# Attention and a two-layer mixer on one core: scores computed in four quarters of the array, a pair's value products in one run, other PSUM banks, and filler products at the start

## The chip, the cores and the metric

The kernel runs on one core of a Trainium2 chip. Times are microseconds (us) of device time for one execution of the whole program. TensorE is called PE here, VectorE DVE, ScalarE ACT, GpSimd POOL; SP is the engine that issues the transfers. Each engine works through its own list of instructions in order.

## The reference

64 heads (8 batches of 8) of 576 positions and 64 dimensions; attention is causal in blocks of 64 positions. Then a mixer over positions and a two-layer network over 512 channels.

```
scores = scale * np.matmul(q, k.transpose(0, 1, 3, 2))
mask = block_i >= block_j                      # blocks of 64 positions
scores = np.where(mask, scores, -1000000000.0)
attn = softmax(scores); out = np.matmul(attn, v)
...
h = xt @ U @ V;  u = x + h.transpose(0, 2, 1)
ch = np.maximum(u @ w_ch1, 0.0) @ w_ch2
return u + ch
```

## The kernel before, in words

The work goes by pairs of heads, 32 pairs in all; four pairs make one batch. The queries of a head are cut into five tiles that end at positions 64, 192, 320, 448 and 576 (tile 0 has 64 queries, tiles 1 to 4 have 128), so tile i sees the first 128i+64 keys. For a pair p the steps are:

- `load_qk`, `load_v`: transfers; POOL scales the keys.
- `scores(p, s)`, twice per pair (s = 0, 1), called a score run here. PE multiplies queries by keys in float32. The two heads of the pair lie in rows 0 to 63 and 64 to 127 of the array, and a run takes tiles 4, 1 and 0 of one head and tiles 3 and 2 of the other, so that both halves work side by side. Tiles 4, 1 and 0 land in `bw` (two PSUM banks), tile 3 in `three`, tile 2 in `two`, a bank each. In tiles 1 to 4 the first 64 queries may not see the last 64 keys; a small bf16 product with the tile `mask` adds a large negative number there. DVE then takes the row maxima (L1215), ACT the exponentials with their sums (L1226).
- `normalise`: DVE inverts the sums, POOL scales the probabilities (L1250).
- `transpose`: PE turns the probabilities (L1293), ACT or DVE copies them out of PSUM (L1264, L1266). One copy in four goes to DVE (`VEC`).
- `apply_v(p, g)`: the value products (L1313) for the positions up to 320 (g = 0) and beyond (g = 1), each a task of its own; ACT copies the result to `xt`.
- `mix`: transposes (L1336), down product (L1351), up product (L1366) and the sum `u` (L1371). The largest |u| of a batch sets its scale (the product named `oneu`).

The network's work is cut in two. `ffn_chunk` (L666, L691) has 2304 products of 288 columns and runs in two banks `bf` between the attention's products; it needs the whole of batch 0 mixed and the first weights converted (DVE and ACT do that from raw words, with two products named `onew`). `block_products` (L915) has 3360 products and starts when the attention is over, because it takes over the attention's banks; its weights are prepared by ACT, DVE and POOL (L768).

What decides the order: every step is recorded with `add(engine, ns, prio, ...)`; `Plan.issue` then plays the tasks through with the costs written in the source and writes each engine's list in the order that this gives. A task starts there when its inputs are there, its engine is free, and each of its PSUM buffers finds a bank in its pool; among the ready ones the lowest `prio` goes first. FFN products have the highest number, so they fill what is left of PE. The attention's pools are `banks_a` (four banks), `banks_w` (`bw`), and for tile 3 of the first four pairs `banks_f` (`bf`), which the FFN uses later.

## Time and profile before

| | us |
|---|---|
| median of 3 runs | 1147.44 (1145.18 to 1148.29) |
| the profiled execution | 1149.23 |
| its span, first to last instruction | 1147.5 |
| first FFN product on PE | 115.3 |
| last product of the attention's last mix | 646.2 |
| last product of the FFN chunks | 737.5 |

The profiled execution took 1.7 us more than its span and 1.8 us more than the median of the runs. The span falls into a start, in which only the attention and the conversion of weights run; a long middle, in which FFN products fill PE between the attention's products; and the block products at the end. Busy times of an engine are unions of its instructions' spans; a PE product is shown from its start to the end of its pipeline, so neighbours overlap, and what a product costs PE is the distance of its start to the next one's.

### The profile page before, as it was taken

The page shows a single profiled execution, that of the slowest core. Times are in us where ns is not written, and L with a number is a line of the kernel's source. Part 1 is how long each engine was busy: PE and PEld are TensorE (multiplying, and loading weights), DVE is VectorE, ACT ScalarE, POOL GpSimd, SP SyncE. Part 2 cuts the span into 40 slices and gives each one's busy share as a digit, 9 for nine tenths or more (in the row PEclk, how much of TensorE's full clock was granted, in tenths as well). Part 3 has the DMA queues.
Part 4 walks back from the last instruction along what each step waited for, and adds up shares of the span by engine and source line. Part 5 has one row for each costly group of instructions (what it writes and reads, how often), then busy time and mean ns, then how long its engine had stood idle before and what let it go on. Part 6 is the DMA issues. An engine that isn't in the chain of part 4 may idle for free.

```text
span 1147.5 us, 24596 instructions
## 1 busy us (share of the span) xinstructions
PE 1096.5 (96%) x9088; PEld 875.1 (76%) x9088; DVE 875.0 (76%) x1946; ACT 653.0 (57%) x1666; POOL 351.0 (31%) x628
## 2 busy tenths in 40 slices
PE   5886998999999999999999999999999999999998
PEld 5665766778777877777878877777777777777777
DVE  4777887778775656567786572399999899999998
ACT  4666766676585756567577552154545554454544
POOL 3433433644563626264656755000000000000000
PEclk8887998999999999999999999999999999999999
DMA  3433553444423232233422431204031231404111
GB/s 106 131 101 98 160 163 107 148 148 122 146 85 105 77 116 75 96 129 115 140 84 63 117 102 47 78 1 125 16 111 52 73 95 31 117 13 120 33 53 43
DMA packets 68264, 107.32 MB, mean 94 GB/s; under 512 B 6896, under 2 KB 50928, under 8 KB 68144
## 3 DMA queue, kind: packets, MB, share of 16 engines
q1 hardware_dynamic: 68144, 105.75, 30.0%
q8 instruction: 72, 1.18, 0.4%
q14 instruction: 48, 0.39, 0.1%
HBM read 76.23 MB, written 29.49 MB: 92 GB/s over the span
## 4 chain that ended last, share of the span: by engine, by line
PE 82%; DVE 7%; ACT 5%; POOL 2%; issue 2%; DMA 1%; SPq 0%; ACTq 0%; POOLq 0%; DVEq 0%
PE bb L915 36%; PE bf L691 11%; PE bf L666 8%; PE ba L1293 7%; PE ba L1313 7%; PE bw L1191 6%; PE ba L1191 3%; DVE mx L1215 3%; ACT p L1226 3%; POOL p L1250 2%; PE ba L1336 1%; PE ba L1351 1%; PE ba L1366 1%; DMA st<-in_U_dram 1%; DMA raw<-in_qk_dram 0%
## 5 line engine op out<-in xcount | busy, mean ns | idle before, releaser
L1250 POOL TENSOR_SCALAR p<-p,rv 64x64 f32<-64x64 f32 (+4 forms) x384 | 187.6, 500 | 149.0 <-DVE rv L1239 58.8
L1215 DVE TENSOR_REDUCE mx<-bw 128x1 f32<-128x576 f32 (+2 forms) x192 | 79.4, 439 | 105.1 <-PE bw L1191 61.4
L915 PE MATMUL bb<-ph,w2h 128*128 128x288 f16 x560 | 151.0, 286 | 0.0
L915 PE MATMUL bb<-ph,w2l 128*128 128x288 f16 x560 | 151.0, 286 | 0.0
L915 PE MATMUL bb<-ph,w1h 128*128 128x288 f16 x560 | 148.7, 286 | 0.0
L915 PE MATMUL bb<-ph,w1l 128*128 128x288 f16 x560 | 148.7, 286 | 0.0
L1191 PE MATMUL bw<-raw 64*128 64x288 f32 (+2 forms) x512 | 132.4, 393 | 14.2 <-ACT p L1226 10.2
L837 ACT CAST ph<-hb 128x576 f16<-128x576 f32 x144 | 84.3, 590 | 82.8 <-PE bb L915 77.1
L915 PEld LDWEIGHTS <-w2h 128*128 128x128 f16 x1120 | 109.6, 98 | 27.5
L1226 ACT ACTIVATE p<-bw,mx 128x576 f32<-128x576 f32 (+2 forms) x192 | 93.4, 489 | 65.3 <-DVE mx L1215 46.8
L915 PEld LDWEIGHTS <-w1h 128*128 128x128 f16 x1120 | 109.6, 98 | 27.4
L915 PE MATMUL bb<-pl,w2h 128*128 128x288 f16 x560 | 123.5, 286 | 0.0
L1293 PE MATMUL ba<-ident,p 128*128 128x128 f32 x704 | 105.8, 284 | 12.7 <-ACT spare L1266 4.4
L915 PE MATMUL bb<-pl,w1h 128*128 128x288 f16 x560 | 114.4, 286 | 0.0
L691 PE MATMUL bf<-hh,w2h 128*128 128x288 f16 x384 | 110.9, 289 | 0.9 <-DVE ot L703 0.7
L1191 PEld LDWEIGHTS bw<-raw 64*128 64x128 f32 x512 | 85.0, 196 | 34.1 <-ACT p L1226 12.2
L691 PE MATMUL bf<-hl,w2h 128*128 128x288 f16 x384 | 110.6, 288 | 0.0
L691 PE MATMUL bf<-hh,w2l 128*128 128x288 f16 x384 | 110.6, 288 | 0.0
L1191 PE MATMUL ba<-raw 64*128 64x448 f32 (+1 forms) x240 | 103.8, 544 | 0.8 <-ACT xt L1266 0.8
L1293 PEld LDWEIGHTS ba<-ident,p 128*128 128x128 f32 x704 | 83.7, 146 | 21.4 <-POOL p L1250 8.3
L666 PEld LDWEIGHTS <-w1h 128*128 128x128 f16 x768 | 74.3, 98 | 23.3 <-issue 5.7
L839 DVE TENSOR_TENSOR pl<-hb,ph 128x576 f16<-128x576 f32 x144 | 91.1, 651 | 1.0
(167 smaller groups left out, 2465.3 us busy)
## 6 DMA issues: line engine op xcount, KB each, us to landing
raw<-in_qk_dram SPq DMA_DIRECT2D x31, 576.0 KB, 3.9
o_d<-ot SPq DMA_DIRECT2D x72, 144.0 KB, 1.8
vr<-in_v_dram SPq DMA_DIRECT2D x32, 320.0 KB, 3.2
ur<-u_d SPq DMA_DIRECT2D x64, 144.0 KB, 2.3
wr<-o_d SPq DMA_DIRECT2D x32, 288.0 KB, 3.0
out_dram<-wr SPq DMA_DIRECT2D x31, 288.0 KB, 2.3
st<-in_w_dram SPq DMA_DIRECT2D x16, 512.0 KB, 3.9
u_d<-ut SPq DMA_DIRECT2D x28, 288.0 KB, 2.3
```

Source lines behind the costliest of these rows:

```text
L666: nc.tensor.matmul(ps[:, :T], w()[wn][:, k, fs], m[k].ap, start=(i == 0), stop=(i == len(ops) - 1))
L691: nc.tensor.matmul(ps[:, :T], w()[wn][:, f, ms], hs[f][x].ap, start=(i == 0), stop=(i == len(ops) - 1))
L837: add("ACT", _act(n * T, True), E, lambda: nc.scalar.copy(h.ap[:, :n, :], x[0]()), [x[1]], [h])
L839: "DVE", _dve(n * T), E, lambda: nc.vector.tensor_sub(l.ap[:, :n, :], x[0](), h.ap[:, :n, :]), [x[1], h], [l],
L915: nc.tensor.matmul(bank[:, i, :T], x()[:, w(k)], p.ap[:, k, :], start=first and n == 0, stop=last and n == len(ops) - 1)
L1191: lambda: nc.tensor.matmul(out(), raw[r, qs], raw[r, S + k0 : S + k1], start=True, stop=not last),
L1215: lambda i=i, mx=mx: nc.vector.tensor_reduce(out=mx[: P if i else 64, i : i + 1], in_=view(i), op=ALU.max, axis=AX.XY if i == 4 else AX.X, ...
L1226: return nc.scalar.activation(out.rearrange("p (j k) -> p j k", j=2) if i == 4 else out, view(i), AF.Exp, bias=mx[:rows, i : i + 1], accum ...
L1250: lambda: nc.gpsimd.tensor_scalar(out=out, in0=x, scalar1=iv, scalar2=1.0, op0=ALU.mult, op1=ALU.mult),
L1293: nc.tensor.transpose(out=to, in_=pt_r[i][h % PB[i]][:, j * P : (j + 1) * P], identity=perm.ap)
L1313: nc.tensor.matmul(bank[64 * s : 64 * s + 64, x:n], vr[:, 5 * s + j, :], pw[s][:, _at(g, j)], start=(j == 0), stop=(j == NK[g] - 1),)
L1336: nc.tensor.transpose(out=ps[:, i, :], in_=xt[:, j * P : j * P + rows], identity=ident.ap)
```

## The change

Four things are changed, and the order follows from them.

1. The score products are cut by blocks of 64 queries. Each block of queries meets only the keys that it may see, and its product lands in PSUM rows 0 to 63 or 64 to 127, so that a run works in four quarters of the array (two heads by two halves of the output rows) instead of two halves. The products with `mask` go; the places that no product writes are filled with the large negative number once, at the start.
2. `apply_v` is one task per pair and takes two banks at once.
3. PSUM: tiles 2 and 3 get a pair of banks `bq` of their own; `banks_a` shrinks from four banks to two. For the first four pairs these two serve as a second pair for tiles 2 and 3 (class `Lent`), and transposes, values and mix use `bf`.
4. Order: scores get a lower priority number by `SL` = 1985, almost one pair; `normalise` is done per score run; `mx`, `ss` and `rv` have four slots; copies of transposes go to DVE only from pair 8 on (`VP`); the second half of the FFN's first weights gets a later priority (`WP2`, `WP4`). Where PE finds nothing ready in the planner's first 130 us and a bank `bf` is free, a product of a zero tile is written into the list (`idle`): bf16, 128 columns, with its own load of weights.

```diff
-PEQ = 1650.0
+PEQ = 1560.0
+PVX = 190.0
+NF = 4
+SL = 1985.0
+WARM = 130e3
+IDLE = 56.0
+VP = 8
...
-WP2, WP3, WP4 = 9000.0, 1000.0, 13000.0
+WP2, WP3, WP4 = 14000.0, 1000.0, 18000.0
...
                 if n is None:
+                    if e == "PE" and now < WARM and idle():
+                        busy[e] = True
+                        heapq.heappush(events, (now + IDLE, 0, -1, e))
                     continue
...
-    banks_a = [psa.tile([P, 512], F32, name=f"ba{i}") for i in range(6 - FB)]
+    banks_a = [psa.tile([P, 512], F32, name=f"ba{i}") for i in range(4 - FB)]
...
+    banks_q = [[psa.tile([P, 512], F32, name=f"bq{i}") for i in (2, 3)]]
+    banks_l = Lent([banks_q.pop(), list(banks_a)], 2 * NF, (banks_q.append, banks_a.extend))
+    banks_a.clear()
+    for x in (banks_w[0][0:64, 0, T + P : T + P + 64], banks_w[0][0:64, 1, S - 64 - T : T]):
+        nc.vector.memset(x, NEG)
...
-        two, three, big = Buf(pool=Rest(banks_a)), Buf(pool=banks_f if p < 4 else Rest(banks_a)), Buf(pool=banks_w)
+        wide, pair = Buf(pool=banks_w), Buf(pool=banks_l if p < NF else banks_q)
...
+            def block(x, n, k0=0, k1=None):
+                r = slice(64 * x, 64 * x + 64)
+                i, c = (n + 1) // 2, 64 * (n > 0 and n % 2 == 0)
+                k1 = 64 * (n + 1) if k1 is None else k1
+                o = view(i)[c : c + 64]
+                o = o[:, k0 // T, : k1 - k0] if i == 4 else o[:, k0:k1]
+                nc.tensor.matmul(o, raw[r, 64 * n : 64 * n + 64], raw[r, S + k0 : S + k1], start=True, stop=True)
+
+            for x in (
+                (a, 7, 0, T), (a, 8, 0, T), (b, 5), (b, 6), (a, 7, T, 512), (a, 8, T, S), (b, 3), (b, 4), (a, 1), (a, 2), (a, 0),
+            ):
+                block(*x)
...
-        copy((g, part) in VEC, n, pr, lambda: pw[:, span], lambda: bank[:, :n], [bank], [b])
+        copy((g, part) in VEC and h >= 2 * VP, n, pr, lambda: pw[:, span], lambda: bank[:, :n], [bank], [b])
...
+        add("PE", cost + PVX, pr, products, [vr, *(y for g in pw for x in g for y in x.parts)], bank, hold=xt.parts)
...
+    def banks_p(p):
+        return banks_f if p < NF else banks_a
...
         for s in range(2):
-            scores(p, s, pr + 10 + 20 * s)
+            scores(p, s, pr + 10 + 20 * s - SL)
+            normalise(p, s, pr + 30)
...
+    def idle():
+        if not banks_f:
+            return False
+        nc.tensor.matmul(banks_f[0][:, 0:P], still, still, start=True, stop=True)
+        return True
```

**Where the lists differ.** PE's list at its start, before: nine float32 products of the zero tile, then the first score run (`raw` holds queries and keys).

```order
L1056 MATMUL bf_90<-zero 128x128 x9
L1191 MATMUL bw<-raw_154 128x288
L1191 MATMUL bf_90<-raw_154 128x448
L1191 MATMUL bw<-raw_154 128x288
L1192 LDWEIGHTS mask
L1192 MATMUL bf_90<-mask 128x64
L1192 LDWEIGHTS mask
L1192 MATMUL bw<-mask 128x64
L1191 MATMUL bw<-raw_154 128x192
L1191 MATMUL ba_95<-raw_154 128x320
```

The same place now: the nine products still stand first, then 103 fillers (L1472, a load and a product each, the last of them shown), then the run.

```order
L1472 LDWEIGHTS zero
L1472 MATMUL bf_90<-zero 128x128
L1218 MATMUL bw<-raw_160 64x288 x2
L1218 MATMUL bq_99<-raw_160 64x384
L1218 MATMUL bq_99<-raw_160 64x448
L1218 MATMUL bw<-raw_160 64x224
L1218 MATMUL bw<-raw_160 64x288
L1218 MATMUL bq_98<-raw_160 64x256
L1218 MATMUL bq_98<-raw_160 64x320
L1218 MATMUL bw<-raw_160 64x128
L1218 MATMUL bw<-raw_160 64x192
L1218 MATMUL bw<-raw_160 64x64
```

The run has 11 products of 64 output rows where it had six of 128 and four of the mask, and 103 fillers moved in ahead of it.

PE's list at the first FFN product, before: the g = 0 half of pair 4's values, apart from its g = 1 half, then the FFN (L666).

```order
L1192 MATMUL ba_97<-mask 128x64
L1313 MATMUL ba_96<-spare,vr_183 64x320 x2
L1313 MATMUL ba_96<-spare,vr_183 64x192 x2
L1313 MATMUL ba_96<-spare,vr_183 64x64 x2
L666 LDWEIGHTS w1h_228
L666 MATMUL bf_91<-uh_123,w1h_228 128x288
```

The same place now: fillers, the last transpose of `xt` of pair 4 (L1364), then the FFN (L692).

```order
L1472 LDWEIGHTS zero
L1472 MATMUL bf_90<-zero 128x128
L1364 MATMUL ba_96<-ident,xt_201 64x128
L692 LDWEIGHTS w1h_238
L692 MATMUL bf_90<-uh_129,w1h_238 128x288
```

What stands on PE ahead of the first FFN product, counted in the lists: before 13 score runs, 130 transposes, five pairs' values, 20 transposes of `xt`, four down and eight up products; now 16 runs, 157 transposes, six pairs' values, 25 transposes of `xt`, four down and eight up products, and all 409 fillers. On ACT 151 instructions stand ahead of the first FFN eviction before, 193 now. At the values of pair 12 both lists have 420 FFN products behind them; at the last up product of the attention the FFN has 1602 of its 2304 products behind it before, 1740 now.

The values of a pair now (pair 0): both halves in one piece, into two banks.

```order
L1337 MATMUL bf_90<-spare,vr_191 64x256 x6
L1337 MATMUL bf_90<-spare,vr_191 64x192 x2
L1337 MATMUL bf_90<-spare,vr_191 64x64 x2
L1337 MATMUL bf_91<-spare,vr_191 64x320 x2
L1337 MATMUL bf_91<-spare,vr_191 64x192 x2
L1337 MATMUL bf_91<-spare,vr_191 64x64 x2
```

The g = 0 half moved up to its g = 1 half; before, the halves of 19 of the 32 pairs stood apart.

## Rows read from the trace of the kernel before

**Rows 1.** The page: PE's line (busy time, share of the span, instructions), and PE's busy tenths and granted clock in tenths in 40 slices of 28.7 us.

```profile
PE 1096.5 (96%) x9088; PEld 875.1 (76%) x9088; DVE 875.0 (76%) x1946; ACT 653.0 (57%) x1666; POOL 351.0 (31%) x628
PE   5886998999999999999999999999999999999998
PEclk8887998999999999999999999999999999999999
```

**Rows 2.** Four stretches of the span: length, busy us and instructions of each engine, granted clock, share of the DMA engines, GB/s.

```profile
0.00:115.30 115.30, 84.05 (x584) 66.42 (x585) 77.46 (x245) 67.45 (x209) 46.25 (x96) 0.85 0.35 109
115.30:200.00 84.70, 78.06 (x639) 60.88 (x639) 70.90 (x193) 57.23 (x163) 31.82 (x63) 0.96 0.46 142
200.00:645.00 445.00, 435.17 (x3799) 349.23 (x3796) 308.45 (x837) 293.03 (x889) 228.09 (x429) 1.00 0.35 109
645.00:1147.50 502.50, 499.22 (x4076) 398.57 (x4073) 418.21 (x674) 235.29 (x405) 44.89 (x42) 1.00 0.23 68
```

**Rows 3.** Lines of the kernel one by one: duration in ns (least, median, most), and the starts of the first and the last: FFN products, up products of the mix, block weights on POOL, and the weight loads of the value products.

```profile
L666 PE MATMUL bf<-uh,w1h x384: 282/286/299, 115.3 to 727.7; 128*128 128x288 f16 x192
L691 PE MATMUL bf<-hl,w2h x384: 284/286/448, 122.7 to 737.5; 128*128 128x288 f16 x192
L1366 PE MATMUL ba<-v,t x64: 288/388/408, 46.5 to 646.2; 96*128 96x288 f32 x64
L768 POOL TENSOR_TENSOR w2l<-spare,w2h x7: 2613/2616/2621, 657.5 to 695.9; 128x1280 f16<-128x1280 f32 x7
L1313 PEld LDWEIGHTS ba<-pw,vr x608: 132/137/138, 41.7 to 634.5; 128*64 128x64 f32 x152
```

**Rows 4.** PE in order of time, a score run in the middle with its neighbours: start, us to the end of the group, line, out and in, rows and columns of the array, shape, count (a float32 product is two entries, one per pass).

```profile
406.21 0.60 PE L1336 MATMUL ba<-ident,xt 128*128 128x128 f32 x4
406.74 0.51 PE L1191 MATMUL bw<-raw 64*128 64x288 f32 x1
406.75 0.64 PE L1191 MATMUL ba<-raw 64*128 64x448 f32 x1
...
408.28 0.41 PE L1191 MATMUL bw<-raw 64*128 64x64 f32 x2
408.62 0.30 PE L691 MATMUL bf<-hh,w2h 128*128 128x288 f16 x1
```

**Rows 5.** PE in order of time, other products in the middle: half a pair's values alone, down products, a whole pair's values, up products, transposes, FFN products.

```profile
202.09 0.27 PE L422 MATMUL ba<-ident,oneu 128*128 128x128 f32 x1
202.30 1.20 PE L1313 MATMUL ba<-spare,vr 128*64 128x320 f32 x12
203.42 0.51 PE L1191 MATMUL bw<-raw 64*128 64x288 f32 x1
...
400.94 0.55 PE L1351 MATMUL ba<-xh,ust 128*64 128x128 f32 x5
401.32 0.40 PE L1351 MATMUL ba<-xl,ust 128*64 128x128 f32 x4
401.56 0.41 PE L1293 MATMUL ba<-swap,p 128*128 128x128 f32 x2
...
402.22 2.94 PE L1313 MATMUL ba<-pw,vr 128*64 128x256 f32 x32
405.09 0.53 PE L1366 MATMUL ba<-v,t 96*128 96x288 f32 x2
405.46 0.30 PE L691 MATMUL bf<-hh,w2h 128*128 128x288 f16 x1
...
418.27 1.94 PE L1293 MATMUL ba<-ident,p 128*128 128x128 f32 x16 [0.18 <-DVE ut L1371]
...
427.29 0.65 PE L666 MATMUL bf<-uh,w1h 128*128 128x288 f16 x4
427.78 0.65 PE L666 MATMUL bf<-uh,w1l 128*128 128x288 f16 x4
```

**Rows 6.** The start in order of time, on PE and ACT: the last zero products and the first score run, ACT's wait for the words of U, and the second score run (in brackets the idle time ahead and what ended it).

```profile
4.62 0.58 PE L1056 MATMUL bf<-zero 128*128 128x128 f32 x2
5.14 0.51 PE L1191 MATMUL bw<-raw 64*128 64x288 f32 x1
...
9.66 0.68 ACT L380 ACTIVATE z<-st 128x128 f32<-128x128 f32 x2 [7.44 <-DMA st<-in_U_dram]
...
12.21 0.85 PE L1191 MATMUL bw<-raw 64*128 64x288 f32 x1 [5.12 <-ACT p L1226]
12.85 0.68 PE L1191 MATMUL bw<-raw 64*128 64x288 f32 x1
...
15.21 0.43 PE L1191 MATMUL bw<-raw 64*128 64x64 f32 x2
```

**Rows 7.** Who PE waited for, first in the stretch 0 to 115.3, then in 115.3 to 645: us in total, times, longest.

```profile
PE bw L1191 <- ACT p L1226: 10.2, 4, 5.1
PE ba L1293 <- POOL p L1250: 6.4, 7, 2.3
PE ba L1293 <- ACT spare L1266: 2.5, 4, 1.2
...
PE bf L666 <- DVE hl L674: 4.1, 6, 0.9
PE ba L1293 <- ACT spare L1266: 2.6, 3, 2.0
```

More of the change, by code (lines that the diff above doesn't have):

```diff
@@ L129, in append, with __init__, __len__, pop @@
         self.pool.append(x)
-class Rest:
-    def __init__(self, pool):
-        self.pool = pool
-    def __bool__(self):
-        return len(self.pool) > 1
-    def pop(self, n):
-        return self.pool.pop(n)
+class Lent:
+    def __init__(self, some, uses, homes):
+        self.free, self.uses, self.homes = list(some), uses, list(zip(some, homes))
+    def __len__(self):
+        return len(self.free)
+    def pop(self, _):
+        x = self.free.pop(0)
+        self.uses -= 1
+        if not self.uses:
+            rest, self.free = self.free, []
+            for y in rest:
+                self.append(y)
+        return x
     def append(self, x):
-        self.pool.append(x)
+        if self.uses:
+            self.free.append(x)
+        else:
+            next(home for y, home in self.homes if y is x)(x)
 ENGINES = ("DVE", "PE", "ACT", "POOL", "SP")
@@ L205, in issue @@
                     new = [b for b in tasks[n][6] if b.ap is None]
-                    if all(b.pool for b in new) and not (port and tasks[n][7]) and not (e == "POOL" and now < held):
+                    if all(len(b.pool) >= sum(x.pool is b.pool for x in new) for b in new) and not (port and tasks[n][7]) and not (e == "POOL" and now < held):
                         break
@@ L1044, in attention_then_mixer @@
     nc.vector.memset(zero.ap, 0.0)
+    still = zero.ap.bitcast(BF16)[:, 0:P]
     ident = buf(fp, [P, P], F32, "ident")
@@ L1179, in view @@
             if i == 4:
[L1180 removed]
+                return wide[:, :, :T]
             if i > 1:
[L1182 to L1195 removed]
@@ L1206, in scores @@
-        add(
-            "PE", PEQ, pr, products, [raw], [big, two, three],
-        )
-        ha, hb = 2 * p + a, 2 * p + b
-        todo = [(ha, 4, big), (ha, 1, big), (ha, 0, big), (hb, 3, three), (hb, 2, two)]
-        for h, i, bank in todo:
-            mx = mx_r[h % 2]
+                return pair[i - 2][:, :w]
+            return wide[:rows, side[i][0], side[i][1] : side[i][1] + w]
+        def products():
+            def block(x, n, k0=0, k1=None):
[9 more added lines that the diff above has]
+                block(*x)
```

163 lines of the change are left out of this document (75 added, 88 removed).

## The prediction

> **What bounds the kernel now.** I read the page first: PE is busy for 96% of the span, and its row of tenths stands at 9 everywhere but in the first four slices, where the granted clock dips too [rows 1]. The table by stretches says how much that is [rows 2]. Up to 115.3 us, where the first FFN product stands [rows 3], PE is busy 84.05 us, idle 31.25 us, and its mean clock is 0.85. From there to 645 it is idle 6.64 + 9.83 = 16.5 us, and in the block products 3.3 us. So there are two regimes: in the start the time hangs on waits, later on the sum of PE's products, because an FFN product always stands ready to fill PE. A microsecond saved on PE after 115.3 is a microsecond of the end; in the start it counts if the FFN begins earlier, or if more of the attention lies behind PE when it begins.
>
> What PE waits for in the start is the exponentials that free `bw` (10.2 us) and POOL's scaling ahead of the transposes (6.4) [rows 7]. The dip of the clock is seen in the second run: PE idles 5.12 us, the next 288 columns take 0.64 us from one pass to the next (12.21 to 12.85), and the run from 12.21 to its last products at 15.21 takes 3.0 us where a run in the middle takes 1.54 (406.74 to 408.28): that is 1.2 GHz against 2.4 [rows 4, 6]. Part of that first wait is ACT standing in front of the words of U until 9.66 [rows 6].
>
> **Prices on PE at full clock.** A run takes 1.97 us: the four transposes ahead cost 0.11 each, so PE is free at 406.65, and the next FFN product starts at 408.62 [rows 4]. Half a pair's values alone (576 columns in each column half) take 1.12 us, a whole pair's (1600 columns) 2.87, so a float32 column costs 1.75/1024 = 1.71 ns and a change of product kind about 0.13 us [rows 5]. Transposes cost (1.94 - 0.28)/15 = 0.11 us, a down product set 0.62, an up product 0.18, an FFN product 0.49/4 = 0.1225 [rows 5].
>
> **Part 1, quarters.** The busier half of the array streams 288 + 288 + 192 + 64 = 832 columns a run, 1.42 us, so 0.55 of the 1.97 is masks, loads and the change at both ends. In quarters the sums are 704, 768, 640 and 768 columns; the longest takes 1.31 us if the four run side by side. With the same 0.55 that is 1.86, without the masks (two of 64 columns at 0.1225/288 per column, 0.05 us) 1.81. Eleven products load more often than six, so I take 1.85, a gain of 0.12. The bounds: 0.2 if all of the masks' cost goes, nothing if the loads show. No row has four quarters at once; two halves by rows are seen in the runs [rows 4], two halves by columns in the values [rows 5].
>
> A rule speaks against this part. In the value products both column halves use all rows, and 32 products with a load of 137 ns each (4.4 us of loads) go by in 2.87 us [rows 3, 5], so loads lie under running products there. The Trainium skill (TensorE: Matmul & The Clock Gate, Part 3) says that a load overlaps running products only where the row group differs, which two quarters of one head do not. By that rule the loads of a head's 7 products, two passes each, would come on top; the trace does not agree where it can be asked. What it would give is rival C below.
>
> **Part 2, values in one run.** It saves 0.13 us where the halves stood apart: 19 of 32 pairs, so about 15 of the 26 left after the start, 2 us.
>
> **Parts 3 and 4, the start.** I price what stands ahead of the first FFN product. Before: 13 x 1.97 + 130 x 0.11 + 5 x 2.9 + 20 x 0.11 + 4 x 0.62 + 8 x 0.18 + 0.3 = 61 us of work in 115.3. Now: 16 x 1.85 + 157 x 0.11 + 6 x 2.9 + 25 x 0.11 + 2.5 + 1.4 + 0.3 = 71.3 us. The 409 fillers come on top: nothing less than 128 columns at the FFN's rate, 0.054 us; a down product of 128 columns costs 0.06 (401.32 to 401.56 for four), a transpose 0.11 [rows 5]. It is nearest to the down product (one pass, own load): 0.06, so 24.5 us; with 0.11 it is 45. The zero products that still stand first end at 5.1 [rows 6]. Sum: 101 us on PE without any wait. The 103 fillers ahead of the first run put it at about 11.3 instead of 5.14; that costs some 2 us, not 6, because ACT could not begin before 9.66 anyway [rows 6].
>
> A page puts a higher price on fillers: the Trainium skill (TensorE: Matmul & The Clock Gate, Back-to-back issue gap) has about 81 ns for a load and a product of 128 columns in a stream; by that they are 33 us and the sum below is 8.6 us larger. No row shows such a pair.
>
> ACT cannot do it much sooner: its 67.45 us for 151 instructions [rows 2] become about 86 for 193, after 9.7 us, so 96 without a wait. Fillers are put where the planner saw PE without work, so waits that it saw are counted in them; what is not is waits that it did not see or had no free `bf` for. Below, none: the FFN starts at 101. Above, all 30 us of today's waits: 131. The nearest row is the stretch from 115.3 to 200, run by the same planner with a full list: 6.64 of 84.7, or 7.8%, 8 us of 101. ACT and the chain of runs are tighter here, so 10: the FFN starts at 111.
>
> **The middle.** 2304 FFN products (282 us) cover the remaining edits, which I cost at nothing: the inverses per run, three copies in four becoming four on ACT until pair 8, later second weights, more slots. Without that cover the copies alone would be 0.6 us each. One thing may cost: the transposes, values and mix of pairs 4 to 31 have two banks instead of four, and the values take both. PE's waits for copies out of PSUM before transposes are 2.6 us in this stretch today [rows 7]; I add 3 us. The end: 564 FFN products, 69 us, are left after the last up product. POOL's last block weight ends at 698.5, 52 us after 646.2 [rows 3], so PE stays covered; before, 702 were left.
>
> **The sum**, against the profiled span of 1147.5: from the first FFN product to the end 1032.2 us remain today. Off come the work now ahead of it, 3 runs (5.9), 27 transposes (3.0), a pair's values (2.9) and five transposes of `xt` (0.5), 12.3 in all; 48 runs at 0.12, 5.8; values, 2; on come 3 for banks. That leaves 1015, and with the start at 111 the span is 1126. The profiled execution took 1.7 more than its span and 1.8 more than the median, so the median would be 1126.
>
> **Rivals.**
>
> A. The start gains nothing: the chain from scores by maxima and exponentials to transposes is as long as before, and fillers push it. For it: in the start DVE and ACT are each busy only 59 to 67% [rows 2], so waits and not work set it, and `bw` is still one. Against: while the clock is down a run takes 3.0 us instead of 1.54 [rows 4, 6], and fillers leave PE no idle time to lose it in. The FFN then begins at 120 (115.3 plus the late first run), and the time is 1135. Fillers at 0.11 would make it 1146.
>
> B, the one on the other side. Two banks: each group of transposes waits for the copy of the group before last, and a copy of 512 columns and its way there is about as long as the group. Price: 26 pairs of 8 groups, 208 waits; at 0.12 us each 25 us, which with the 3 already counted taken off eats the whole gain of 21; from there on it decides. For it: that wait is there today with four banks [rows 7]. Against: FFN products stand between most groups. With 0.13, 27 us instead of 3, the time is 1150; from 0.14 on it is slower by more than can be mistaken.
>
> C. The quarters of one head do not run side by side. Then a half streams 512 + 576 + 128 + 192 + 64 = 1472 columns, 2.52 us, a run is 3.05 and 64 runs cost 77 us more than I count: 1203. The value products speak against it. By the rule above, the trace disagreeing, it has a small chance.
>
> D. Everything goes as the list says, with hardly a wait in the start (FFN at 101) and runs at 1.8: 1113.
>
> **How the numbers follow.** Forecast (1117 to 1134) 0.58, A 0.18, D 0.10, B 0.10, C 0.04. What a measurement of this kernel can tell from no change is 0.3%, 3.4 us. Faster by more: the forecast, D, and nearly all of A, together 0.86; the same: the upper end of A and the lower part of B, 0.06; slower: the rest of B, and C, 0.08. For 8 in 10 the range reaches from D's lower side, 1110, to A's upper end, 1144.
>
> **What would show it.** The first FFN product at 105 to 117 and a granted clock in the start above 0.95; runs of 1.8 to 1.9 us from the product ahead to the one behind; fillers 0.06 apart; PE idle from there to 645 at 15 to 22 us; the last FFN chunk product 20 us earlier, and the block products as long as now. Wrong would be: runs near 2 us or more, fillers at 0.08 or more with the FFN at 120, or waits of transposes on copies of more than 10 us.

## The result and the profile after

The changed kernel takes 1104.62 us (median of 4 runs, 1103.98 to 1106.05), the kernel before in the same session 1147.87: a ratio of 0.963 (95% interval 0.961 to 0.965). It is 43 us faster where 21 were forecast, and lies below the range of 1110 to 1144. The profiled execution took 1103.98 us with a span of 1102.2. In three of the experiments one execution of four ran to several milliseconds (5127 us in halves and masks, 6392 in the cut halves, 2801 in the early weights without the first fillers); it is left out of the medians below, which with it would be 1125.1, 1124.67 and 1096.68.

The page of the kernel after: PE's line, its busy tenths and its granted clock in 40 slices of 27.6 us.

```profile
PE 1068.4 (97%) x9881; PEld 853.2 (77%) x9881; DVE 847.3 (77%) x1807; ACT 660.0 (60%) x1682; POOL 351.9 (32%) x628
PE   8879899899999999999999999999999999999998
PEclk9999999999999999999999999999999999999999
```

Its stretches, cut at the first FFN product as in [rows 2]: length, busy us and instructions of each engine, clock, DMA share, GB/s.

```profile
0.00:115.60 115.60, 100.47 (x1201) 80.95 (x1202) 79.84 (x249) 85.02 (x264) 59.41 (x121) 1.00 0.40 127
115.60:200.00 84.40, 78.25 (x756) 61.45 (x755) 72.42 (x195) 65.24 (x193) 38.01 (x77) 1.00 0.51 159
200.00:615.00 415.00, 405.89 (x3982) 324.56 (x3980) 282.82 (x700) 278.38 (x833) 222.45 (x402) 1.00 0.36 111
615.00:1102.20 487.20, 483.80 (x3950) 386.24 (x3947) 412.25 (x665) 231.34 (x395) 32.04 (x30) 1.00 0.23 68
```

Lines of the kernel after (duration in ns least/median/most, first and last start): FFN products, the fillers, and loads of score products.

```profile
L692 PE MATMUL bf<-uh,w1h x384: 283/286/298, 115.6 to 681.5; 128*128 128x288 f16 x192
L717 PE MATMUL bf<-hl,w2h x384: 284/286/286, 123.1 to 691.3; 128*128 128x288 f16 x192
L1472 PE MATMUL bf<-zero x409: 216/219/314, 5.7 to 114.8; 128*128 128x128 bf16 x137
L1218 PEld LDWEIGHTS bq<-raw x480: 129/133/133, 11.7 to 572.3; 64*64 64x64 f32 x160
```

The first FFN product did not move: 115.6, before 115.3 [rows 3]. The clock in the start is now 1.00 where it was 0.85 [rows 2], and PE idles there 15.1 us where it idled 31.25, and still the FFN starts when it did. All of the gain lies behind it: from the first FFN product to the end 986.6 us pass, 1032.2 before; in this lies the work of a pair that the start now does in the same time. The last product of an FFN chunk starts at 691.3 where it started at 737.5 [rows 3].

PE of the kernel after in order of time: fillers and the first score run, then a run in the middle with its neighbours.

```profile
5.65 6.08 PE L1472 MATMUL bf<-zero 128*128 128x128 bf16 x103
11.67 0.46 PE L1218 MATMUL bw<-raw 64*64 64x288 f32 x2
...
306.42 0.65 PE L692 MATMUL bf<-ul,w1h 128*128 128x288 f16 x4
307.00 0.46 PE L1218 MATMUL bw<-raw 64*64 64x288 f32 x2
307.29 0.41 PE L1218 MATMUL bw<-raw 64*64 64x288 f32 x2
307.54 0.41 PE L1218 MATMUL bw<-raw 64*64 64x224 f32 x2
...
308.13 0.38 PE L1218 MATMUL bw<-raw 64*64 64x64 f32 x3
308.45 0.44 PE L1337 MATMUL ba<-pw,vr 128*64 128x256 f32 x2
```

From its first product to the next kind a run takes 1.45 us; before it took 1.88 (406.74 to 408.62) [rows 4]. All 48 runs behind the first FFN product take 1.45, 69.7 us in all; before, 51 runs took 96.8, 1.90 each.

**Where the 45.6 us behind the first FFN product come from.** The pair that moved ahead of it: 12.3, as priced in the prediction. 48 runs at 1.90 - 1.45: 21.4. The values of a pair, summed from each product's start to the next one's: 74.5 us for 832 products, where 80.9 for 864 gives 77.9 for as many: 3.4. The clock between 115 and 200, 0.96 before [rows 2] and 1.00 now: 0.04 x 84.7 = 3.4, an estimate, of which some 0.9 is already in the 1.90 of the runs (51 at 1.88 are 95.9). PE idle up to the last up product: 15.3 where it was 16.5, 1.2. That is 41.7; 3.9 us stay without a place of their own. The transposes may hold most of it: 0.116 us each where they took 0.121 (78.1 us for 675, 85.2 for 702), 3.8 us, though part of that is the clock again.

### The profile page after: what moved, and what is told of

Same layout as the page of the kernel before. It is cut to its first block, busy times and chain, and to the rows that moved or that the text cites. A ratio compares the mean times of both kernels' runs of the same rounds, so it can differ in the third digit from the quotient of the medians.

```text
span 1102.2 us, 25896 instructions
## 1 busy us (share of the span) xinstructions
PE 1068.4 (97%) x9881; PEld 853.2 (77%) x9881; DVE 847.3 (77%) x1807; ACT 660.0 (60%) x1682; POOL 351.9 (32%) x628
## 4 chain that ended last, share of the span: by engine, by line
PE 76%; DVE 9%; ACT 6%; POOL 4%; DMA 3%; issue 2%; POOLq 0%; ACTq 0%; SPq 0%; DVEq 0%
PE bb L941 37%; PE bf L692 10%; PE bf L717 10%; PE ba L1317 6%; ACT p L1242 4%; PE bw L1218 3%; DVE mx L1231 3%; PE ba L1337 3%; POOL p L1263 2%; PE bq L1218 2%; DMA raw<-in_qk_dram 2%; PE ba L1364 1%; PE bf L1472 1%; PE ba L1379 1%; DVE z L390 1%
## 5 line engine op out<-in xcount | busy, mean ns | idle before, releaser
L1231 DVE TENSOR_REDUCE mx<-bw 128x1 f32<-128x576 f32 (+2 forms) x192 | 78.1, 438 | 79.9 <-PE bw L1218 48.3
L941 PEld LDWEIGHTS <-w2h 128*128 128x128 f16 x1120 | 109.6, 98 | 27.7
L1242 ACT ACTIVATE p<-bw,mx 128x192 f32<-128x192 f32 (+2 forms) x192 | 93.3, 489 | 59.9 <-DVE mx L1231 57.3
L1218 PE MATMUL bw<-raw 64*64 64x288 f32 (+4 forms) x896 | 97.0, 345 | 4.1 <-POOL z L409 1.5
L1317 PE MATMUL ba<-ident,p 128*128 128x128 f32 x616 | 92.5, 275 | 4.3 <-DVE tz L1383 1.7
L1218 PE MATMUL bq<-raw 64*64 64x384 f32 x480 | 90.4, 469 | 0.0
L717 PEld LDWEIGHTS <-w2h 128*128 128x128 f16 x768 | 75.4, 98 | 18.1 <-issue 0.2
L692 PEld LDWEIGHTS <-w1h 128*128 128x128 f16 x768 | 74.2, 98 | 17.5
L1218 PEld LDWEIGHTS bw<-raw 64*64 64x64 f32 x896 | 65.0, 132 | 19.4 <-issue 7.7
```

The costliest lines, as they stand in the source:

```text
L692: nc.tensor.matmul(ps[:, :T], w()[wn][:, k, fs], m[k].ap, start=(i == 0), stop=(i == len(ops) - 1))
L717: nc.tensor.matmul(ps[:, :T], w()[wn][:, f, ms], hs[f][x].ap, start=(i == 0), stop=(i == len(ops) - 1))
L941: nc.tensor.matmul(bank[:, i, :T], x()[:, w(k)], p.ap[:, k, :], start=first and n == 0, stop=last and n == len(ops) - 1)
L1218: nc.tensor.matmul(o, raw[r, 64 * n : 64 * n + 64], raw[r, S + k0 : S + k1], start=True, stop=True)
L1231: lambda i=i, n=n: nc.vector.tensor_reduce(out=mx[: P if i else 64, n : n + 1], in_=view(i), op=ALU.max, axis=AX.XY if i == 4 else AX.X, n ...
L1242: return nc.scalar.activation(out.rearrange("p (j k) -> p j k", j=2) if i == 4 else out, view(i), AF.Exp, bias=mx[:rows, n : n + 1], accum ...
```

## The experiments

The first theory was that the surplus lies in the score runs, because quarters lose less around their products (Q); its rivals, that it is the masks alone (M), or the clock that the fillers hold up (F). All ratios are to the kernel before, run in the same session.

### What a score run is made of

**Halves and masks again, all else as changed.**

```diff
-PEQ = 1560.0
+PEQ = 1650.0
...
-            for x in (
-                (a, 7, 0, T), (a, 8, 0, T), (b, 5), (b, 6), (a, 7, T, 512), (a, 8, T, S), (b, 3), (b, 4), (a, 1), (a, 2), (a, 0),
-            ):
-                block(*x)
...
+            for x in (a4[0], b3[0], a5[0], b3[1], a5[1], a1[0], b2[0], a1[1], narrow[0], b2[1]):
+                x()
```

> The changed kernel with its score products in two halves again and with the mask products, all else kept. Theory Q (a run in quarters takes 1.45 us where one in halves took 1.90, by the distance of starts in the two traces, and the 48 runs behind the first FFN product carry that to the end): 1104.6 + 48 x 0.45 = 1126, up to 1133 if the 16 runs of the start count too. Rival W (the gain beyond the forecast came from fewer waits and the order): 1104.6 + 48 x 0.12 = 1110.

Measured: 1124.04 us, ratio 0.9775 (0.9748 to 0.9802); 49 runs behind the first FFN product at 1.88. The quarters are worth 1124.04 - 1104.62 = 19.4 us (17 by the ratios; 20.5 behind the first FFN product in the two traces), and the rest of the change some 24. So Q holds and W falls. Not all else is as changed: the planner's cost of a run, `PEQ`, is that of halves again, and the order moves with it (the FFN begins at 117.2 with one run and a pair's values less ahead of it). With halves the time is about that of the forecast, which had 5.8 for the quarters: the rest gave some 8 us more than it had.

**The kernel before without its mask products.** The scores of keys that a query may not see are left in.

```diff
-            last = k1 == w and i > 0
+            last = False
...
-            for x in (a4[0], b3[0], a5[0], b3[1], a5[1], a1[0], b2[0], a1[1], narrow[0], b2[1]):
+            for x in (a4[0], b3[0], a5[0], a1[0], b2[0], narrow[0]):
```

> The kernel before without the mask products: the last 64 keys of each tile's first 64 queries are left unmasked, so this part of the computation is left out; queues and banks stay. Theory M (most of the 0.55 us of a run beyond its columns is the four mask products with their loads): runs of 1.6 us and 51 x 0.3 us off behind the first FFN product, 1132. Rival N (the masks cost their columns only, 0.05 us a run, and the quarters win by how loads and passes interleave): 1145.

Measured: 1133.67 us, ratio 0.9876 (0.9841 to 0.991). The median run behind the first FFN product takes 1.66 us. The two traces side by side show what a mask costs. First the halves with masks, PE in order of time: the passes of the longer half, a mask product, the two passes of 192 columns behind it, the next kind.

```profile
303.35 0.51 PE L1222 MATMUL bw<-raw 64*128 64x288 f32 x1
...
303.69 0.40 PE L1222 MATMUL bw<-raw 64*128 64x288 f32 x1
...
303.94 0.65 PE L1222 MATMUL bw<-raw 64*128 64x288 f32 x2
...
304.42 0.19 PE L1223 MATMUL bw<-mask 64*128 64x64 bf16 x1
304.45 0.41 PE L1222 MATMUL bw<-raw 64*128 64x192 f32 x1
...
304.69 0.32 PE L1222 MATMUL bw<-raw 64*128 64x192 f32 x1
...
305.23 0.40 PE L1403 MATMUL ba<-v,t 96*128 96x288 f32 x1
```

The same products in the kernel before without masks:

```profile
304.97 0.51 PE L1191 MATMUL bw<-raw 64*128 64x288 f32 x1
...
305.31 0.40 PE L1191 MATMUL bw<-raw 64*128 64x288 f32 x1
...
305.56 0.64 PE L1191 MATMUL bw<-raw 64*128 64x288 f32 x2
...
306.04 0.32 PE L1191 MATMUL bw<-raw 64*128 64x192 f32 x1
...
306.20 0.49 PE L1191 MATMUL bw<-raw 64*128 64x192 f32 x3
306.62 0.53 PE L1366 MATMUL ba<-v,t 96*128 96x288 f32 x2
```

Behind a mask product the two passes of 192 columns stand 0.24 us apart (304.45 to 304.69); without it 0.16 (306.04 to 306.20). The mask's own columns take 0.03 (304.42 to 304.45). So a mask costs 0.11, two of them on the longer half 0.22: that is 1.88 - 1.66. I had priced their columns only, 0.05.

The loads of weights show where the 0.08 comes from. The two loads for the passes of 192 columns behind the mask product, then, without masks, the load for the first of these passes:

```profile
304.42 0.19 PEld L1222 LDWEIGHTS bw<-raw 64*128 64x128 f32 x1
...
304.53 0.19 PEld L1222 LDWEIGHTS bw<-raw 64*128 64x128 f32 x1
```

```profile
305.80 0.19 PEld L1191 LDWEIGHTS bw<-raw 64*128 64x128 f32 x1
```

In both traces no load begins before the pass ahead of it in its half does. Without masks that pass is a long one: the load begins with it at 305.80 and is over when its own pass begins at 306.04. A mask product is through after 0.03: the load that begins with it at 304.42 still runs when its pass begins at 304.45, the next load follows 0.11 behind it, and 0.11 - 0.03 is the 0.08. In all 49 runs with masks the first pass of 192 columns lasts 0.406 us, in the 51 without them 0.322. This is read from the rows; no run of its own tests it.

The other 0.21, from 1.66 to 1.45: the longest quarter streams 768 columns where the half streams 832, 0.11. The pass that opens a run begins together with its own load; it lasts 0.51 in halves where a later one of 288 columns lasts 0.40 (304.97 and 305.31), and two of them 0.46 against 0.41 in quarters (307.00 and 307.29), whose loads are shorter (131 ns, not 187): 0.05. The rest, 0.05, is lost behind the last columns: 1.66 - 1.42 - 0.10 = 0.14 in halves, 1.45 - 1.31 - 0.05 = 0.09 in quarters.

**More loads, in quarters and in halves.** Four of the eleven products of a quarter run cut in two; then, in the kernel of halves and masks, tile 4's two products cut in two.

```diff
-                (a, 7, 0, T), (a, 8, 0, T), (b, 5), (b, 6), (a, 7, T, 512), (a, 8, T, S), (b, 3), (b, 4), (a, 1), (a, 2), (a, 0),
+                (a, 7, 0, T), (a, 8, 0, T), (b, 5, 0, 192), (b, 6, 0, 224), (b, 5, 192), (b, 6, 224), (a, 7, T, 512), (a, 8, T, S), (b, 3, 0, 128), (b, 4, 0, 160),
+                (b, 3, 128), (b, 4, 160), (a, 1), (a, 2), (a, 0),
```

```diff
-            a4, a5 = (part(a, 4, wide[:, j, :T], j * T, j * T + T) for j in range(2))
+            a4, c4, a5, c5 = (part(a, 4, wide[:, j, x : x + 144], j * T + x, j * T + x + 144) for j in range(2) for x in (0, 144))
```

> The changed kernel with four of the eleven products of each run cut in two, so 15 products and 30 loads of weights a run in place of 22; the columns are the same. A load takes 131 ns in the trace. If loads lie under the running products of other quarters, a run stays at 1.45 to 1.55 us and the time at 1104 to 1108. If they show, 8 x 0.131 us a run come on top, 67 us in 64 runs: 1172; if half of them show, 1138.

> The changed kernel with the scores in halves and mask products again (1125.1 us, 1.88 us a run), and tile 4's two products cut in two each, so that the longer half has two products, four loads, more for the same columns. If loads show in halves, where every load meets a running product in its own rows, a run takes 4 x 0.131 = 0.52 us more, 2.4 us, and the time is 1155; if half of each shows, 2.14 and 1140. If loads are hidden in halves as they are in quarters, the run stays below 1.95 and the time at 1124 to 1128, and the gain of quarters beyond the masks has another cause.

Measured: 1104.46 us (ratio 0.9627, 0.9608 to 0.9646) with every run behind the first FFN product at 1.46; and 1124.40 (0.9804, 0.9788 to 0.9821) with runs at 1.89, where the uncut halves take 1.88. The loads of the cut quarter run:

```profile
L1218 PEld LDWEIGHTS bq<-raw x960: 128/133/134, 11.5 to 572.8; 64*64 64x64 f32 x192
```

30 loads of 131 ns are 3.9 us of loading in a run of 1.46: they lie under running products, in quarters as in halves. So "the loads show" falls for these cuts. But every piece here is long: in halves a pass of 144 columns takes 0.12 us and the loads of two passes need start only 0.11 apart. These runs do not say that a load never shows; by the rows above it does behind a mask product and at the opening of a run.

### The values

**Values as two tasks again.**

```diff
...
-        apply_v(p, pr + 60)
+            apply_v(p, g, pr + 50 + 10 * (1 - g))
```

> The changed kernel with the value products in two tasks again, each with one bank. Theory from the traces (26 pairs behind the first FFN product went from 80.9 us for 864 products to 74.5 for 832, so 3.5 us for the 26 pairs): 1108. Rival (one bank at a time lets transposes go on, so the merged form costs waits that it saves in changes of products): 1102 to 1105.

Measured: 1106.52 us (0.9635, 0.962 to 0.965), 1.9 more than the changed kernel, which these intervals do not tell from nothing; the order differs too (the FFN begins at 106.8, with two runs and a pair's values less ahead of it). On PE the form shows: the values of the 27 pairs behind the first FFN product take 81.8 us where 27 at the changed kernel's price take 77.4.

### What sets the start

**No fillers.** `WARM` = 0 in place of 130e3.

> The changed kernel without the filler products. Theory F (the fillers keep the clock up, and a run at half clock takes 3.0 us in the chain that sets the start): granted clock of the start back to 0.85, first FFN product 5 to 12 us later, 1110 to 1117. Rival G (the start hangs on DVE, ACT, POOL and transfers; fillers only stand in the way, above all the first 103): first FFN product at 112 to 116, 1101 to 1105.

**No fillers ahead of the first run only.**

```diff
-                    if e == "PE" and now < WARM and idle():
+                    if e == "PE" and 5700.0 < now < WARM and idle():
```

> The changed kernel without the 103 fillers ahead of the first score run; the other 306 stay. The changed kernel took 1104.6 us, without any filler 1098.8. If the late first run (11.67 us instead of 5.8) is what the fillers cost, the FFN starts 3 to 5 us before the 115.6 of the changed kernel and the time is 1099 to 1101. If it is the fillers later on, which stand in front of transposes that become ready, the time stays at 1103 to 1106. The granted clock of the start falls below 1.00 in either case, since PE idles between the first two runs.

**Fillers that take no time in the plan**, so that the order of all other instructions is that of the kernel without fillers.

```diff
...
                 if n is None:
-                    if e == "PE" and now < WARM and idle():
-                        busy[e] = True
-                        heapq.heappush(events, (now + IDLE, 0, -1, e))
+                    if e == "PE" and 5700.0 < now < WARM and gap is None:
+                        gap = now
                     continue
+                if e == "PE" and gap is not None:
+                    for _ in range(int((now - gap) / IDLE)):
+                        idle()
+                    gap = None
```

> The order of the kernel without fillers (1098.8 us, FFN at 116.7, 981.5 us behind it), in which fillers take no time in the plan: they are written into PE's gaps after 5.7 us of planner time only, 470 ahead of the first FFN product. If fillers do in the start what the full clock is worth and only shift the plan behind it, the FFN starts at 110 to 112, 981 to 983 us follow, and the time is 1092 to 1095. If a PE that is earlier only waits again for DVE, ACT and POOL in the middle, 986 us follow as with the 306 fillers, and the time is 1097 to 1100. If 470 fillers stand in the way of transposes that have become ready, the FFN starts at 115 or later and the time is 1097 to 1103.

Measured: 1098.79 us without fillers (0.9568, 0.9547 to 0.9589), 1099.07 without those ahead of the first run (0.958, 0.9558 to 0.9602), 1100.41 with fillers outside the plan (0.9602, 0.9582 to 0.9622). The stretch up to the first FFN product, first without fillers:

```profile
0.00:116.70 116.70, 87.52 (x792) 62.59 (x793) 79.50 (x249) 85.05 (x264) 58.50 (x121) 0.91 0.40 125
```

The same order with 470 fillers:

```profile
0.00:116.60 116.60, 102.46 (x1261) 84.36 (x1262) 79.56 (x249) 85.09 (x263) 59.17 (x121) 1.00 0.40 126
```

And without those ahead of the first run, in the order that the other 306 make:

```profile
0.00:111.10 111.10, 94.77 (x1098) 75.09 (x1099) 79.52 (x249) 84.90 (x264) 59.14 (x121) 1.00 0.42 132
```

Without any filler the clock of the start is 0.91, not 0.85, the FFN begins 1.1 us later, not 5 to 12, and the time is 5.8 shorter: F falls, and the time is below what its rival had, too. Without the first fillers the time is the one expected, but the clock, expected below 1.00, stays at 1.00.

In one and the same order the clock rises from 0.91 to 1.00, and the FFN begins 0.1 us earlier. The 16 score runs, from their first product to the next kind, fall from 41.5 to 24.6 us; 9 us of that are waits inside and behind them, the rest is clock. All of PE's work but the fillers falls from 87.5 to 75.2 us, and 470 fillers bring 27.3. So this pair does not show that a full clock is worth nothing: PE gets ahead by it, and the fillers take the lead back. The same group of eight transposes, first without fillers, then with them:

```profile
44.38 1.19 PE L1317 MATMUL bf<-ident,p 128*128 128x128 f32 x8 [0.68 <-ACT pw L1290]
```

```profile
39.73 1.00 PE L1475 MATMUL bf<-zero 128*128 128x128 bf16 x15 [0.67 <-ACT pw L1293]
40.57 1.04 PE L1320 MATMUL bf<-ident,p 128*128 128x128 f32 x8
```

PE has come 5 us ahead in the second trace (transposes shortly before these start at 36.74, without fillers at 41.72). But when ACT's copy is done, 15 fillers start where the transposes started, and the lead shrinks to 3.8; at 101.84 both traces begin the same values. What the runs show is that fillers together with the clock that they hold gain nothing here, the third reading of the expectation: 470 fillers stand in the way. My first reading, that the start would fall to 110 to 112 without a change of order, was wrong.

The 103 fillers ahead of the first run cost 4.5 us of start (115.6 to 111.1, in the same order) and 5.5 of the time. And the order with its fillers, 306 in the one and 470 in the other, moves the FFN's start by 5.5 us (111.1 against 116.6), while behind it 986.1 us follow in the one and 981.4 in the other, with PE idle 14.8 and 10.6 us up to the last up product. The two cancel, so the three kernels end within 1.6 us of each other.

**One pair of banks for score tiles 2 and 3 from the start.**

```diff
-    banks_l = Lent([banks_q.pop(), list(banks_a)], 2 * NF, (banks_q.append, banks_a.extend))
-    banks_a.clear()
+    banks_l = Lent([banks_q.pop()], 2 * NF, (banks_q.append,))
```

> The changed kernel with one pair of banks for score tiles 2 and 3 from the first pair on; the second pair of the start is gone. 14 runs and five pairs' values then stand ahead of the first FFN product, where there were 16 and six: 2 x 1.45 + 2.9 + 5 x 0.11 = 6.3 us of work move behind it. If the start is set by the sum of work, the FFN starts 6 us earlier and the time stays at 1104 to 1106. If it is set by the conversion of weights and the chain of the first batch, the FFN starts at 115 to 117 all the same and the time is 1110 to 1112.

Measured: 1111.42 us (0.9681, 0.9656 to 0.9706). 14 runs and five pairs' values stand ahead of the FFN, which starts only at 123.7:

```profile
0.00:123.70 123.70, 105.84 (x1150) 83.95 (x1150) 78.05 (x239) 81.20 (x249) 54.16 (x114) 0.90 0.36 116
```

The second pair of banks is worth 8.1 us of start and 6.3 us of work done in it; 6.8 us of the time, since the middle has 10.4 us of idle time here and 15.3 in the changed kernel. The time is that of the second reading of the expectation, but the FFN begins later than either reading had it. Of the parts of the change that were undone, this one shortens the start most.

**Other parts of the order, undone one by one:** `SL` = 0 (scores late); the second half of the first weights early (`WP2, WP3, WP4` = 9000, 1000, 13000, as before); and, without the fillers ahead of the first run, `VP` = 0 (copies on DVE from the first pair on).

> The changed kernel with the scores back at their own pair's place in the order (SL = 0). If early scores are worth something, it is waits of transposes on the probabilities in the middle: before the change these were 1.2 + 1.1 us, so the time rises by no more than 2 to 4 us by them, plus up to 6 us for the two runs and the pair of values that fall behind the first FFN product: 1107 to 1114. If they are worth nothing, the FFN starts 6 us earlier with 6 us less behind it, and the time is 1103 to 1106.

> The changed kernel with the second half of the FFN's first weights at its earlier place in the order. 14 runs and five pairs' values then stand ahead of the first FFN product in place of 16 and six. If the later place is worth something, it is PE's idle time at 115 to 200 us, which was 6.6 us before the change with a granted clock of 0.96 and is 6.0 with 1.00 after it: 3 to 6 us come back there and the time is 1108 to 1112. If it is worth nothing, the time is 1102 to 1106.

> The kernel without the fillers ahead of the first run, with one copy of transposes in four on DVE from the first pair on (VP = 0). 14 runs and five pairs' values stand ahead of the first FFN product in place of 16 and six. Some 16 copies of 0.57 us, 9 us, go from ACT to DVE in the start. If ACT (84.9 us busy of 111.1) sets the start, the FFN begins 5 to 9 us earlier, at 102 to 106, and the time is 1095 to 1100; if DVE sets it, the FFN begins at 112 to 118 and the time is 1103 to 1110.

Measured: 1104.05 (0.9625, 0.9601 to 0.9648), 1102.17 (0.9606, 0.9587 to 0.9625), and 1105.17 (0.9633, 0.9589 to 0.9678) against 1099.07 with `VP` = 8. Early scores gain nothing in the time: without them the FFN begins at 116.5 with the same 6.3 us of work less ahead of it, so they do shorten the start, but the middle then idles 9.4 us and not 15.3. The later weights lose 2.4 us, less than these intervals tell apart, but about the same again in the pair of kernels further down. Copies kept off DVE gain some 6, with a wide interval, and they gain it in the start: without them the FFN begins at 111.0 in place of 111.1, with 11.6 us less work on ACT (73.3 us busy), but two runs and a pair's values less stand ahead of it, and 992.6 us follow, 6.5 more.

**Whose work, then?** A third slot for queries and keys (with fillers outside the plan), which takes away the transfer that POOL waits for; and, in the kernel without the fillers ahead of the first run, row maxima over 64 keys only in the first six pairs.

```diff
...
-    raw_r = ring(ep, 2, [P, 2 * S], F32, "raw")
+    raw_r = ring(ep, 3, [P, 2 * S], F32, "raw")
...
-        raw = raw_r[p % 2]
+        raw = raw_r[p % 3]
...
```

```diff
-                    out=mx[: P if i else 64, n : n + 1], in_=view(i), op=ALU.max, axis=AX.XY if i == 4 else AX.X,
+                    out=mx[: P if i else 64, n : n + 1],
+                    in_=view(i) if p >= 6 else view(i)[:, 0:1, 0:64] if i == 4 else view(i)[:, 0:64],
+                    op=ALU.max, axis=AX.XY if i == 4 else AX.X,
```

> The same with a third slot for queries and keys (raw), so that POOL no longer waits for a transfer that may only start when the scores of two pairs before are done: 4.25 us at 82 to 86 us in the start. If that wait holds the first batch's mix, the FFN starts 2 to 4 us earlier than with two slots, at 107 to 109, and the time is 1090 to 1093. If the conversion of weights on DVE and ACT holds it, the FFN starts where it did and the time stays at 1093 to 1096, with some us either way from another order in the middle.

> The kernel without the fillers ahead of the first run (1099.1 us, FFN at 111.1, 986.1 behind it), in which the row maxima of the first six pairs are taken over the first 64 keys only, which every query sees; the softmax is the same up to its shift. The order is unchanged. A run's five maxima take about 0.76 + 0.62 + 0.54 + 0.35 + 0.2 = 2.4 us on DVE now and five of 0.2 then: 1.4 us a run, 17 us over twelve runs. If the chain from scores by maxima to exponentials, or DVE's sum of work, sets the start, the FFN begins at 98 to 104 and the time is 1086 to 1092. If ACT, POOL or PE set it, the FFN begins at 109 to 111 and the time is 1097 to 1099.

Measured: 1103.56 (0.962, 0.9604 to 0.9636) with the FFN at 117.5, in place of 116.6; and 1095.04 (0.9538, 0.9519 to 0.9557) with the FFN at 107.0. POOL's waits for queries and keys, first with two slots, then with three:

```profile
POOL raw L1181 <- DMA raw<-in_qk_dram: 10.9, 3, 4.4
```

```profile
POOL raw L1181 <- DMA raw<-in_qk_dram: 10.5, 3, 4.4
```

The third slot did not take the wait away, since the order that the planner writes then asks for the data sooner as well; so that run decides nothing about the transfer. Short maxima, in an unchanged order:

```profile
0.00:107.00 107.00, 93.93 (x1097) 74.69 (x1098) 65.61 (x249) 84.33 (x263) 58.87 (x121) 1.00 0.43 137
```

13.9 us less on DVE bring the FFN forward by 4.1: less than a third of what was taken off DVE was on the path.

**Together:** early second weights without the fillers ahead of the first run, and the same with short maxima.

> Two edits that were faster apart: the earlier second weights (1102.2 us, FFN at 108.8, 988.7 behind it) and no fillers ahead of the first run (1099.1 us, 4.5 us less start). If they add, the FFN begins at 104 to 105, 988 to 989 us follow, and the time is 1095 to 1098. If the conversions of weights set the start and not the first run's time, the FFN begins at 107 to 109 and the time is 1099 to 1102.

> Earlier second weights, no fillers ahead of the first run (1096.7 us, FFN at 103.5), and short maxima in the first six pairs. If DVE's work is worth what it was in the other order, the FFN begins at 99 to 100 and the time is 1092 to 1093. If ACT (79.9 us busy of 103.5, with 9.7 before it can begin) leaves no more room, the FFN begins at 102 to 103.5 and the time is 1095 to 1097.

Measured: 1096.17 us (0.954, 0.9517 to 0.9564) with the FFN at 103.5 and 987.9 us behind it: the two edits add. With short maxima 1093.36 (0.952, 0.9493 to 0.9547), the FFN at 101.7; the intervals of the two overlap. In this order the same DVE work is worth 1.8 us of start, not 4.1. The fastest kernel of the study is 11 us ahead of the changed one; of these, 8 come from fewer fillers and earlier weights, and 3 from maxima over fewer keys, which keep the exponentials in range only while the scores stay small.

What sets the start is thus not one engine's sum of work. Taking 13.9 us from DVE moves it by 1.8 or 4.1; a second pair of score banks moves it by 8, and the order of the lists with its fillers by 5. It is a chain that goes from engine to engine. In the changed kernel the chain that ended last has, within the first 115.6 us, these shares (the view breaks the line off):

```profile
by line: ACT p L1242 14.8%; DVE mx L1231 10.1%; POOL p L1263 9.1%; PE bf L1472 7.8%; PE bw L1218 6.4%; issue 5.3%; DMA raw<-in_qk_dram 4.3%; ACT spare L1290 4.2%; PE bf L1083 3.6%; PE bq L1218 3.4%; DVE z L390 3.0%; DVE wr L398 2.5%; PE bf 
```

No line holds more than 15%, and the fillers (L1472) hold 9 us, more than the score products into `bw`. How each list is ordered decides which waits lie on the chain; which of them a further edit would shorten stays open.

## Why the prediction was wrong, point by point

- **What bounds the kernel.** Right for the stretch behind 115: PE is busy for 98% of it [rows 2], and microseconds saved on it there came off the end (19.4 us in the time for 21.1 on PE, 49 runs of 1.88 against 1.45). Half right for the start: waits do set it, but I then counted it as PE's work plus waits.
- **Part 1, the step that failed.** "With the same 0.55": I kept what a run loses around its columns and changed only the columns. The run went from 1.88 to 1.45, a gain of 0.43 where 0.12 was forecast and 0.2 was the bound. Of the 0.55, masks were 0.22 (I counted 0.05, their columns; the rest is loads that such a short product does not cover), and 0.10 more went at the two ends of the run. The row for it was there: in [rows 4] columns explain 1.42 of 1.97, and I never asked what the remaining half microsecond was before I carried it over. The bound "0.2 if all of the masks' cost goes" rested on the same price. This term alone is 15.6 us of the miss by the traces (21.4 against 5.8), 13.6 by the run with halves (19.4). "Eleven products load more often than six" took the loads the wrong way round: the loads of quarters are the shorter ones, and only those behind a mask and at the opening of a run show.
- **The rule against it.** The prediction weighed the Trainium skill's page (TensorE: Matmul & The Clock Gate, Part 3), by which a load overlaps products only where the row group differs, and kept it at 4 in 100. It fell: quarters of one head share their rows, and 30 loads a run instead of 22 moved a run by 0.01 us. By the rows of loads above, what decides here is how long the pass ahead lasts, not whether the rows differ.
- **Part 2.** Forecast 2 us, measured 3.4 on PE in the traces. Right in kind; the 1.9 us of the run with two tasks are not clear of noise.
- **The start.** Forecast 111, measured 115.6, the clock as forecast. The sum of PE's work held, 100.5 for 101, though not part by part: 16 runs took 24.1 and not 29.6, the 157 transposes 22.2 and not 17.3, the 409 fillers 25.5, 0.062 each, for 24.5 at 0.06. By the 81 ns of the Trainium skill (TensorE: Matmul & The Clock Gate, Back-to-back issue gap) the fillers would have been 33 us; the trace disagrees. What failed is the idle time, 15.1 us where I added 10, and in it "some 2 us, not 6" for the 103 fillers ahead of the first run: they cost 4.5 of start. I set the first run's late start against the 9.66 at which ACT can begin, and left out that the run itself and DVE's maxima stand between the two. ACT's first exponentials with these fillers and without them:

```profile
14.39 0.74 ACT L1242 ACTIVATE p<-bw,mx 128x576 f32<-128x576 f32 x1 [4.84 <-DVE mx L1231]
```

```profile
9.98 0.73 ACT L1242 ACTIVATE p<-bw,mx 128x576 f32<-128x576 f32 x1
```

  That 111.1 comes out without them does not save the method: in another order 12.3 us less of PE's own work and 27.3 us of fillers left the start where it was, and 13.9 us less on DVE alone moved it, so a sum over PE's list was the wrong account. Rival A's mechanism is what happened, at 115.6 and not at 120; its time of 1135 did not, because runs and middle gave more.
- **The middle.** I added 3 us for two banks in place of four. PE's waits in the changed kernel from 115.6 to 615 (us in total, times, longest):

```profile
PE ba L1317 <- DVE tz L1383: 5.1, 7, 1.3
PE ba L448 <- ACT xt L1290: 2.0, 3, 1.0
PE ba L1317 <- ACT spare L1290: 1.1, 1, 1.1
```

  The transposes' waits for copies, 2.6 before [rows 7], are 1.1, so rival B fell. New is the wait for the bank that the mix's `tz` is read from, 5.1 us, more than the 3 that I added for two banks; others of [rows 7] went, and the sum is 1.2 us less. Not forecast at all: the clock between 115 and 200, which was 0.96 [rows 2], is 1.00, worth 3.4 us by the estimate above. The fillers are not what holds it there: without any of them it is 1.00 in that stretch too.
- **The end.** Right: the 3360 block products, each from its start to the next one's, take 411.8 us in both traces, and PE idles 3.4 us there, 3.3 before.
- **The sum.** 1147.5 became 1102.2, not 1126: the 23.8 us between are runs 15.6, the middle's waits 4.2 (1.2 less where 3 more were forecast), the clock 3.4, values 1.4, the 3.9 without a place, less 4.6 for the start; these give 23.9. Rival C fell at once; D, with runs at 1.8 and the FFN at 101, missed on both numbers and came nearest in time, by luck.

## What to carry to other kernels

Before a remainder (0.55 us of a run that its columns don't explain) is carried over into the new form, find out what it is made of: leaving out one kind of product on the chip, or comparing the distance of the same two passes with and without it ahead, would have shown half of this gain (0.22 of 0.43). Where a chain through several engines sets a stretch, price a part by what the chain waits for and not by the sum of one engine's list: 13.9 us less on DVE were worth 1.8 or 4.1 us here, and fillers for the clock nothing, because they also stand in front of work that is ready. A filler that takes time in the planner reorders everything behind it; two orders of the same kernel, with 306 and 470 fillers, differed by 5 us at either end.

## What the runs showed of the hardware that was not expected

- Four quarters of the array run side by side at the columns' own rate: 1.45 us for 2880 columns of two passes each, the longest quarter 1.31 by the price of [rows 5], with 22 loads of 131 ns under them.
- A product of 0.03 us between longer ones costs 0.11: the load for the float32 pass behind it begins only with it (304.42), the next load 0.11 later, and the second pass comes 0.08 later than without it (0.24 against 0.16).
- A load and a bf16 product of 128 columns in a row of 103 take 6.0 us from the first start to the run behind them, 0.058 each.
